# Attention followed by a max-out feed-forward: other wait points for the casting loads and for w_out, and a new planned order

## The chip, the cores and the metric

The kernel runs on one core of one Trainium2 chip. The core has a matrix engine (TensorE, PE in the profile), a vector engine (VectorE, DVE), a scalar engine (ScalarE, ACT), a general engine (GpSimd, POOL) and an engine that issues transfers (SyncE, SP). Each runs its own list of instructions in order; between lists they wait for each other through semaphores. Transfers between the chip's memory and the on-chip memory are issued from SP's, ACT's or POOL's list and run on 16 DMA engines. The metric is the time of one execution on the device in microseconds (us); lower is better.

## What is computed

Four batches, eight heads, 768 positions, head size 64. Three of the eight heads attend to all earlier positions; the other five see the first 4 positions and a window of 64. The heads' kinds are data (`is_retrieval`), so the kernel sorts the heads at run time. The joined heads (3072 x 512) go through a feed-forward with two up projections, of which the larger value is kept, and one down projection. The reference, cut:

```python
scores = scale * np.matmul(q, k.transpose(0, 1, 3, 2))
stream_keep = causal & (is_sink | in_win)
mask = np.where(retr[0, :, 0, 0, None, None], full_mask, stream_mask)
scores = np.where(mask[None, :, :, :], scores, -1000000000.0)
a = np.exp(scores - np.max(scores, axis=-1, keepdims=True))
a = a / (np.sum(a, axis=-1, keepdims=True) + 1e-09)
attn_out = np.matmul(a, v)
x = attn_out.transpose(0, 2, 1, 3).reshape(B * S, H * D)
g = np.maximum(x @ w1, x @ w2)
return g @ w_out
```

## The kernel before

**Tiling.** Each batch is cut into two halves of 384 positions, so there are eight half-batches (b, hf). Heads go in pairs: four pairs per half, one of two full heads, one mixed, two of streaming heads. Two heads of size 64 share the 128 rows of TensorE.

**Attention of one half.** q, k and v arrive as float32 in one of three landing slots (`ld`). q and k are cast to bfloat16 (`qb`, `CAST_QK`), turned on TensorE against an identity matrix (L813) and copied out (`qk`); v is cast (`vb`, `CAST_V`). TensorE makes scores (list S, L1027, with mask terms by L996 for the first half only), ACT takes the exponential (`at`, L1046), DVE multiplies masks (L1065), TensorE makes the weighted sums (list W, L1090), and DVE divides by the row sums (`x`, L1117). `x` is turned on TensorE for batch 0 (list TX, L1210) and by a transposing transfer later (`xt`, L1229).

**Feed-forward.** max(h1, h2) is written as max(h1 - h2, 0) + h2. So the kernel makes `w12` = w1 - w2 (L1246, `sub`), the up product x·w12 (list F, L1301), its positive part `g` (L1325, L1327), and then the output as g·w_out + x·(w2·w_out) in one accumulation (L1351). For that it needs `w2o` = w2·w_out: w2 is cast (`w2b`), turned on TensorE (list P, L1262), copied out (`w2t`), and multiplied with w_out (list P2, L1280). P2 works quarter by quarter: quarter c of w_out meets quarter c of the turned w2, for the k chunks 0 to 2 in the order of the quarters, then chunk 3 for all quarters.

**Loads of the front.** `LOADS` names the order: A and B are q and k of the two halves of batch 0, Av and Bv their v (three pieces each, by position), w20 and w21 the halves of w2, w10 and w11 those of w1. These are issued by SP. wo0 to wo3 are the quarters of w_out; they are cast on their way and issued by POOL. `load_down` (L696) makes each of them wait for an earlier load, `flow[-1 - PACE:len(flow) - PACE]` (L725): the list `flow` holds the earlier SP loads, and PACE is how far back from its end the awaited one lies. Before the wo quarters there stands a one-element copy on POOL (L701, tile `landed`), which is what waits. w1 uses the landing slot that A has left, and so waits for A's casts.

**The last batch.** Batch 3 is not cast by an engine. `load_pair` (L630) issues from POOL, for each pair and head, a casting load of q, k and v (24 in all, L648); q and k are then turned by a transposing transfer (L662). Ahead of the first stands again a one-element copy on POOL (L645) that waits for the load named by `BEHIND` = (half, kind) of batch 2; kind 1 is k, 2 is v.

**The order.** Nothing runs in program order. Each operation has a cost for every engine that could do it, operands and a rank (`RANK`; for batch 0 with `FRONT` and `FRONT_STEP` added; a shift by `STEP` for each half and `FF_STEP` for the feed-forward). While the kernel is built, a planner (`Order.run`, L206) plays the operations through in modelled time, gives each to the engine that would end it first (with a `BIAS` in us against an engine), and writes the instructions in that order. TensorE's work is in lists of fixed inner order (`PE_LISTS`); between lists it takes the first that is ready, a `MARGIN` after it became ready, and, if nothing is, a product on a zero tile (L514, tile `warmer`) up to `WARM_UNTIL`. Scores of a half may begin once the weighted sums of pair `S_AFTER` of the previous half have begun (L1146).

```python
behind = loads[b - 1, BEHIND[0], BEHIND[1]][-1:] if BEHIND else []
wo_in[c] = load_down(c, flow[-1 - PACE:len(flow) - PACE])
deps.append(first_w[(b, 0, S_AFTER) if hf else (b - 1, 1, S_AFTER)])
return begins + o.costs[e2] + o.bias.get(e2, 0.0)
```

Of the kernel before, what the change touches and what calls it, by code (L numbers as in the profile page):

```python
# [132 lines left out]
class Order:  # L133
# [256 lines left out]
CAST_QK = {'POOL': 0.46, 'DVE': 0.27, 'ACT': 0.4}  # L390
CAST_V = {'POOL': 0.3, 'DVE': 0.26, 'ACT': 0.26}
RANK = {
    'cast': -0.9, 'vcast': 14.25, 'unturn': 5.45, 'mix_k': 2.0, 'mix_v': -15.1, 'exp': -2.35,
    'mask': -2.15, 'norm': -12.35, 'take_x': -2.05, 'turn': -22.0, 'w2b': -17.35, 'sub': -9.15,
    'w2t': -3.85, 'wob': 0.35, 'w2o': -6.05, 'relu': 7.1, 'load': 6.6, 'out': -9.7, 'h2': 7.4,
    'table': -10.6, 'vload': 14.1,
}
NLD = 3
NQB = 4
# [8 lines left out]
PE_LISTS = ('TX', 'W', 'S', 'TK', 'TQ', 'P', 'H', 'P2', 'F')  # L408
PLACES = (0, 1, 2, 0, 1, 2, 0, 1, 2, 0, 1, 2, 0, 1, 2, 0, 1, 2, 0, 1, 2, 0)
SECOND_UP = False  # L410
LOADS = ('A', 'B', 'Av', 'w20', 'wo0', 'wo1', 'wo2', 'wo3', 'w10', 'w21', 'w11', 'Bv')
BIAS = {'DVE': 0, 'ACT': 0}
BIAS_MIX = {}
W2B_BEHIND = True
NORM = {'DVE': 0.35}
TURNED_BY_DMA = ()
DMA_TURN = 0.25
PACE = 1
W2O_EARLY = 3
X_LAST = ((0, 0),)  # L420
BIASED = ((0, 0),)
# [15 lines left out]
    0.22, 'six': 0.37,  # L437
}
SPARE = {}
STEP = 0.5  # L440
FF_STEP = -8.1
S_AFTER = 3
S_RUN = 2
S_REST = 1
ENTER_S = 0.1
# [2 lines left out]
COLD_UNTIL = 7.5  # L448
WARM_SHARE = 0.9
SHARE = {'S': 0.45, 'W': 0.8}  # L450
MARGIN = {'W': 0.5, 'S': 2.0, 'F': 0.2, 'TQ': 2.0}
X_MARGIN = 0.4
FRONT = (
    {'mix_k': -15.0, 'mask': 45.1, 'unturn': -38.9, 'exp': 16.6, 'vcast': 17.6, 'cast': -78.7,
    'norm': 6.4}, {'vcast': 14.0, 'unturn': -14.2, 'exp': 51.8, 'mask': 26.2, 'norm': -7.5,
    'mix_k': 24.9, 'cast': 21.2},
)
FRONT_STEP = (31.9, 11.4)
UNTURN_BIAS = ({}, {'ACT': 2.0})
SHARED = 0.89  # L460
UP_PARTS = 2
BY_ACT = {}
V_QUEUES = ()
BEHIND = (1, 2)


def tile_three_full_heads(
# [12 lines left out]
    ident, bias, smask = tab[:, 0:128], tab[:, 128:1152], tab[:, 1152:1920]  # L480
# [39 lines left out]
    T = {}  # L520

    def copy(e, out, in_):
        if e == "ACT":
            nc.scalar.copy(out=out, in_=in_)  # L524
        else:
            eng[e].tensor_copy(out=out, in_=in_)  # L526
# [146 lines left out]
    def load_up(name, src, c):  # L673

        if name not in T:
            s, old, tenants[name] = slot()
            staged_old[name] = old
            T[name] = lds[:, s].rearrange("p t h c -> p (t h c)")[:, 0:KC * d_ff] \
                .rearrange("p (c f) -> p c f", f=d_ff)
        n = d_ff // UP_PARTS  # L680

        by_act = name[:2] + str(c) in BY_ACT

        def emit(_):
            queues["ACT" if by_act else "SP"].dma_start(
                out=T[name][:, :, c * n:c * n + n],
                in_=src.rearrange("(c p) f -> p c f", p=128)[:, :, c * n:c * n + n],
            )
        return dma(
            2.097 / UP_PARTS, emit, [order.given(BY_ACT[name[:2] + str(c)])] if by_act else (),  # L690
            old=staged_old[name], rate=RATE["w"] if UP_PARTS == 4 else RATE["w half"],
            parts=1536 // UP_PARTS, grain=180.0 / UP_PARTS, rank=-9.0 if by_act else 0.0,
            by="ACT" if by_act else "SP",
        )

# [15 lines left out]
    slot_of, tenants, bias_in, table_in, staged_old, half_old, place_of = {}, {}, [], [], {}, {}, {}  # L711
    w1_in, w2_in, wo_in, flow = {}, {}, {}, []
    for what in LOADS:
        kind, c = what[:2], int(what[2:]) if what[:1] == "w" else 0
        if what[0] in "ABCD":
            kinds = (2,) if what[1:] else (0, 1)
            of = divmod("ABCD".index(what[0]), 2)
            load_half(*of, kinds)
            flow += loads[(*of, kinds[-1])]
            for n, o in enumerate(loads[(*of, kinds[-1])]):  # L720
                last = (n if kinds[-1] == 2 or of not in LONG else NT - 1) * D
                row = 64 if kinds[-1] == 1 and of in SIX else 0
                place_of[o] = row, lds[row:row + 1, slot_of[of], kinds[-1], 0, last:last + 1]
        elif kind == "wo":
            wo_in[c] = load_down(c, flow[-1 - PACE:len(flow) - PACE])  # L725
        else:
            got, src = (w1_in, w1) if kind == "w1" else (w2_in, w2)
            got[c] = load_up(kind + "f", src, c)
            flow.append(got[c])
            place_of[got[c]] = 0, T[kind + "f"][0:1, 0, c * d_ff // UP_PARTS:c * d_ff // UP_PARTS + 1]  # L730
    registers = order.given(REGISTERS)
    bias_in.append(order.given(MASKS_MADE))

# [154 lines left out]
    def prepare(b, hf, p):  # L888
# [7 lines left out]
        else:  # L896
# [4 lines left out]
            for hh in range(2):  # L901
                for lo, hi in ((0, 1), (1, 2)) if (b, hf) in SPLIT and (b, hf) not in SIX else ((0, 2),):
# [336 lines left out]
    def prep_weights():  # L1239
        sub_ops, w2b_ops, w2t_ops, w2o_ops = [], [], [], []  # L1240
        n = d_ff // 4
        for c in range(4):
            at = slice(c * n, c * n + n)
            sub_ops.append(op(
                {"DVE": 1.15},
                lambda e, at=at: eng[e].tensor_tensor(  # L1246
                    out=w12[:, :, at], in0=T["w1f"][:, :, at], in1=T["w2f"][:, :, at], op=ALU.subtract
                ),
                [w1_in[c * UP_PARTS // 4], w2_in[c * UP_PARTS // 4]], tag=f"sub{c}", rank=RANK["sub"], port=("POOL",),
            ))  # L1250
            w2b_ops.append(op(
                {"DVE": 0.61, "ACT": act(1024)},
                lambda e, at=at: copy(e, w2b[:, :, at], T["w2f"][:, :, at]), [w2_in[c * UP_PARTS // 4]],
                tag=f"w2b{c}", rank=RANK["w2b"], port=("DVE",),
            ))
            key = ("pw", c)

            def emit(_, c=c, key=key):
                pw = bank(key, BF16)
                for e in range(2 * KC):  # L1260
                    fc = 2 * c + e // KC
                    nc.tensor.transpose(  # L1262
                        pw[:, e * 128:e * 128 + 128],
                        w2b[:, e % KC, fc * 128:fc * 128 + 128], ident,
                    )

            def take(e, c=c, key=key):
                copy(e, w2t[:, 2 * c:2 * c + 2].rearrange("f c k -> f (c k)"), bank(key, BF16))
            o = pe("P", mm(*[128] * 2 * KC), emit, [w2b_ops[c]], claims=[(key, 1)])
            w2t_ops.append(op({"DVE": 0.62, "ACT": act(1024)}, take, [o], frees=[key], tag=f"w2t{c}", rank=RANK["w2t"]))  # L1270
        leaves("w2f", range(3), w2b_ops + sub_ops)
        leaves("w1f", range(3), sub_ops)
        steps = [(c, kc) for c in range(4) for kc in range(W2O_EARLY)]
        steps += [(c, kc) for kc in range(W2O_EARLY, KC) for c in range(4)]
        for c, kc in steps:
            key = ("pw2", kc)

            def emit(_, kc=kc, key=key, c=c):
                for fc in (2 * c, 2 * c + 1):
                    nc.tensor.matmul(  # L1280
                        bank(key), lhsT=w2t[:, fc, kc * 128:kc * 128 + 128], rhs=wob[:, fc, :],
                        start=(fc == 0), stop=(fc == FC - 1),
                    )
            o = pe(
                "P2", mm(512, 512), emit, [w2t_ops[c], wo_in[c]], claims=[(key, 1)] if c == 0 else [],
            )
            if c == 3:
                w2o_ops.append(op(
                    {"DVE": 0.6, "ACT": act(512)},
                    lambda e, kc=kc, key=key: copy(e, w2o[:, kc], bank(key)), [o], frees=[key],  # L1290
                    rank=RANK["w2o"],
                ))
        return sub_ops, list(wo_in.values()), w2o_ops
# [468 lines left out]
```

## Time and profile before

| | |
|---|---|
| median of 3 runs | 180.99 us (180.62 to 182.13) |
| the profiled execution | 180.24 us |
| its span | 178.6 us, 4964 instructions |
| granted TensorE clock | 0.997 |
| read from memory, written | 25.17 MB, 6.29 MB |
| DVE, ACT, POOL busy | 106.3, 129.5, 39.5 us |

The span is the time from the first to the last instruction; the profiled execution is 1.6 us longer than it. A row of a timeline or of the chain begins with the start and the length in us, then the engine, the line, the operation, what it writes and reads, and in brackets the idle time before it and what ended it. "q" behind an engine's name means its issuing part. A matmul's busy time overlaps the next one's, so the chain's lengths, and not the busy times, say how long a group held TensorE.

### The profile page before, as it was taken

The page shows a single profiled execution, that of the slowest core. Times are in us where ns is not written, and L with a number is a line of the kernel's source. Part 1 is how long each engine was busy: PE and PEld are TensorE (multiplying, and loading weights), DVE is VectorE, ACT ScalarE, POOL GpSimd, SP SyncE. Part 2 cuts the span into 40 slices and gives each one's busy share as a digit, 9 for nine tenths or more (in the row PEclk, how much of TensorE's full clock was granted, in tenths as well). Part 3 has the DMA queues.
Part 4 walks back from the last instruction along what each step waited for, and adds up shares of the span by engine and source line. Part 5 has one row for each costly group of instructions (what it writes and reads, how often), then busy time and mean ns, then how long its engine had stood idle before and what let it go on. Part 6 is the DMA issues. An engine that isn't in the chain of part 4 may idle for free.

```text
span 178.6 us, 4964 instructions
## 1 busy us (share of the span) xinstructions
PE 171.1 (96%) x1824; PEld 106.6 (60%) x1843; DVE 106.3 (60%) x319; ACT 129.5 (73%) x285; POOL 39.5 (22%) x75
## 2 busy tenths in 40 slices
PE   7898999999999999999999999999999999999991
PEld 7865985466746747666555655564465566545560
DVE  5487994699797999898673466664044176400000
ACT  3589897489599999899975996583283988425430
POOL 6313600050002605039997510000000000000000
PEclk9999999999999999999999999999999999999998
DMA  4999999999998999969999999991310511412022
GB/s 122 333 312 217 389 197 301 347 274 321 204 266 222 335 214 255 322 191 85 134 192 126 210 158 116 225 240 34 117 62 0 147 62 61 92 71 111 4 87 98
DMA packets 72529, 32.37 MB, mean 181 GB/s; under 512 B 53938, under 2 KB 67506, under 8 KB 72498
## 3 DMA queue, kind: packets, MB, share of 16 engines
q1 hardware_dynamic: 52448, 28.45, 63.0%
q0 software_dynamic: 19904, 3.41, 29.0%
q8 instruction: 16, 0.26, 0.6%
q14 instruction: 15, 0.12, 0.3%
q10 hardware_dynamic: 146, 0.13, 0.2%
HBM read 25.17 MB, written 6.29 MB: 176 GB/s over the span
## 4 chain that ended last, share of the span: by engine, by line
PE 93%; DVE 2%; issue 2%; ACT 1%; POOL 0%; DVEq 0%; ACTq 0%; POOLq 0%
PE ps L1351 35%; PE ps L1301 23%; PE ps L1027 10%; PE ps L1090 8%; PE ps L514 6%; PE ps L813 5%; PE ps L1280 4%; PE ps L996 1%; PE ps L1262 1%; PE ps L1210 1%; DVE vx L526 1%; DVE qk L526 1%; ACT qb L524 0%; DVE at L1065 0%; DVE x L1117 0%
## 5 line engine op out<-in xcount | busy, mean ns | idle before, releaser
L1046 ACT ACTIVATE at<-ps 128x512 bf16<-128x512 f32 (+2 forms) x134 | 64.3, 583 | 3.4 <-PE ps L1027 3.0
L1301 PE MATMUL ps<-xt,w 128*128 128x384 bf16 x256 | 46.1, 326 | 0.0
L1351 PE MATMUL ps<-wob,g 128*128 128x512 bf16 (+1 forms) x195 | 45.5, 370 | 0.2
L524 ACT COPY ot<-ps 128x512 f32<-128x512 f32 (+1 forms) x22 | 12.6, 573 | 28.0 <-PE ps L1351 28.0
L1301 PEld LDWEIGHTS <-w 128*128 128x128 bf16 x256 | 23.5, 98 | 14.7 <-issue 0.2
L1065 DVE TENSOR_TENSOR at<-at,tab 128x1024 bf16<-128x1024 bf16 (+5 forms) x49 | 24.2, 503 | 13.1 <-ACT at L1046 12.7
L1351 PEld LDWEIGHTS <-g 128*128 128x128 bf16 x200 | 18.6, 98 | 19.1 <-issue 0.2
L1325 ACT ACTIVATE g<-ps 128x384 bf16<-128x384 f32 x49 | 24.2, 507 | 5.2 <-PE ps L1301 4.7
L1351 PE MATMUL ps<-w2o,xt 128*128 128x512 bf16 (+1 forms) x89 | 23.6, 370 | 0.6
L1090 PEld LDWEIGHTS <-at 128*128 128x128 bf16 x477 | 19.4, 97 | 7.2 <-DVE at L1065 0.7
L1117 DVE TENSOR_TENSOR x<-ps,rez 128x192 f32 x64 | 22.7, 355 | 1.6
L1090 PE MATMUL ps<-vb,at 128*128 128x65 bf16 x387 | 21.1, 193 | 0.3 <-DVE at L1065 0.3
L1027 PE MATMUL ps<-qk 64*128 64x128 bf16 (+1 forms) x330 | 19.5, 228 | 0.1
L1027 PEld LDWEIGHTS <-qk 64*128 64x128 bf16 x330 | 12.3, 94 | 10.8 <-issue 8.2
L1327 DVE TENSOR_SCALAR g<-ps 128x384 bf16<-128x384 f32 x15 | 8.1, 552 | 11.2 <-PE ps L1301 10.9
L514 PE MATMUL ps<-warmer 128*128 128x128 bf16 x146 | 13.4, 252 | 1.2 <-POOL warmer L1695 1.2
L526 POOL CAST vb<-ld 128x192 bf16 x15 | 6.8, 493 | 33.6 <-DMA ld<-in_v_dram 32.4
L1351 PEld LDWEIGHTS <-xt 128*128 128x128 bf16 x100 | 8.8, 97 | 8.1 <-issue 0.2
L813 PE MATMUL ps<-tab,qb 128*128 128x128 bf16 x144 | 11.3, 221 | 1.2 <-ACT qb L524 0.5
L526 DVE CAST qb<-ld 128x384 bf16 (+1 forms) x34 | 11.0, 375 | 2.0 <-DMA ld<-in_q_dram 1.2
L514 PEld LDWEIGHTS <-warmer 128*128 128x128 bf16 x146 | 11.2, 116 | 1.6 <-POOL warmer L1695 1.2
L526 DVE COPY qk<-ps 128x384 bf16<-128x384 bf16 (+1 forms) x17 | 10.8, 666 | 2.1 <-PE ps L813 1.9
(72 smaller groups left out, 160.6 us busy)
## 6 DMA issues: line engine op xcount, KB each, us to landing
out_dram<-ot SPq DMA_DIRECT2D x23, 256.0 KB, 2.8
ld<-in_q_dram SPq DMA_DIRECT2D x6, 768.0 KB, 7.0
ld<-in_k_dram SPq DMA_DIRECT2D x6, 768.0 KB, 7.5
ld<-in_v_dram SPq DMA_DIRECT2D x18, 256.0 KB, 6.9
ld<-in_moe_w_dram SPq DMA_DIRECT2D x4, 1024.0 KB, 12.8
wob<-in_moe_w_out_dram POOLq DMA_DIRECT2D x4, 256.0 KB, 9.1
ld<-in_q_dram POOLq DMA_DIRECT2D x8, 96.0 KB, 7.8
ld<-in_k_dram POOLq DMA_DIRECT2D x8, 96.0 KB, 7.7
```

Of the source, the lines that this page charges most:

```text
L514: nc.tensor.matmul(banks[e][:, 0:128], lhsT=warm, rhs=warm, start=True, stop=True)
L524: nc.scalar.copy(out=out, in_=in_)
L526: eng[e].tensor_copy(out=out, in_=in_)
L813: nc.tensor.transpose(to[:, i], qbs[:, T["qb", n, hf] % NQB, t, i].rearrange("p h d -> p (h d)"), ident)
L1027: nc.tensor.matmul(to.rearrange("p (i c) -> p i c", c=128), lhsT=lhsT, rhs=q_of(n, i, m)[rows], start=bk not in under, stop=True, skip_gro ...
L1046: nc.scalar.activation(out=at[:, bk, 0:w], in_=bank(("ps", b, hf, t), part=bk)[:, 0:w], func=ACT.Exp, scale=scale,)
L1065: eng[e].tensor_tensor(out=at, in0=at, in1=tbl, op=ALU.mult)
L1090: nc.tensor.matmul(po[:, hh, i - NT * hf, :], lhsT=ats[:, T["at", b, hf, t] % NAT, bk, e * 128:(e + 1) * 128], rhs=rhs, start=first, stop= ...
L1117: nc.vector.tensor_tensor(out=xs[:, (2 * b + hf) % NX, :, bass.ds(heads[2 * p + hh], 1), :], in0=po[:, hh, :, 0:D].unsqueeze(2), in1=z[:, ...
L1301: nc.tensor.matmul(bank(key)[:, 0:HALF], lhsT=w[:, kc, fc * 128:(fc + 1) * 128], rhs=xts[:, (2 * b + hf) % NXT, :, kc, :], start=(kc == 0) ...
L1325: nc.scalar.activation(out=g, in_=ph, func=ACT.Relu)
L1351: nc.tensor.matmul(bank(key)[:, cols], lhsT=lhsT, rhs=(w2o if kind == "x" else wob)[:, c, cols], start=(e == 0), stop=(e == len(steps) - 1),)
```

## The change

It changes constants of the planner and waits, and adds a switch that is off (`W2_ROWS = False`: w2 loaded by rows instead of columns).

- The order of the front's loads: wo0 and wo1 are now named ahead of w20, w21 and w10, and wo2 and wo3 behind them. With PACE 2 instead of 1 the awaited load changes too. Before, all four waited for the last v piece of A (`flow` = A's k, B's k, three pieces of A's v, w20; the one before the last). After, wo0 and wo1 wait for the first v piece of A, and wo2 and wo3 for w20.
- SP's own order stays: w20, w21, w10, w11 and Bv, where w10 and w11 wait for A's landing slot and so came behind w21 before as well.
- BEHIND goes from (1, 2) to (1, 1): batch 3's casting loads wait for the load of k in the second half of batch 2. There k is followed by two v pieces.
- BIAS: the casts of batches 1 and 2 count 2.5 us more on DVE and ACT.
- S_AFTER, STEP, FF_STEP, MARGIN, RANK, FRONT, FRONT_STEP and UNTURN_BIAS get other values, so that the planner writes another order.

```diff
 RANK = {
-    'cast': -0.9, 'vcast': 14.25, 'unturn': 5.45, 'mix_k': 2.0, 'mix_v': -15.1, 'exp': -2.35,
-    'mask': -2.15, 'norm': -12.35, 'take_x': -2.05, 'turn': -22.0, 'w2b': -17.35, 'sub': -9.15,
-    'w2t': -3.85, 'wob': 0.35, 'w2o': -6.05, 'relu': 7.1, 'load': 6.6, 'out': -9.7, 'h2': 7.4,
-    'table': -10.6, 'vload': 14.1,
+    'cast': -0.7, 'vcast': 17.15, 'unturn': 4.4, 'mix_k': 0.3, 'mix_v': -16.2, 'exp': -2.7,
+    'mask': -2.3, 'norm': -10.5, 'take_x': -3.3, 'turn': -22.15, 'w2b': -16.6, 'sub': -10.25,
+    'w2t': -6.05, 'wob': -0.15, 'w2o': -7.05, 'relu': 6.15, 'load': 7.7, 'out': -11.0, 'h2':
+    7.3, 'table': -8.8, 'vload': 14.85,
 }
...
-LOADS = ('A', 'B', 'Av', 'w20', 'wo0', 'wo1', 'wo2', 'wo3', 'w10', 'w21', 'w11', 'Bv')
-BIAS = {'DVE': 0, 'ACT': 0}
+LOADS = ('A', 'B', 'Av', 'wo0', 'wo1', 'w20', 'w21', 'w10', 'wo2', 'wo3', 'w11', 'Bv')
+BIAS = {'DVE': 2.5, 'ACT': 2.5}
...
-PACE = 1
+PACE = 2
...
-STEP = 0.5
-FF_STEP = -8.1
-S_AFTER = 3
+STEP = 1.25
+FF_STEP = -7.8
+S_AFTER = 2
...
-MARGIN = {'W': 0.5, 'S': 2.0, 'F': 0.2, 'TQ': 2.0}
+MARGIN = {'W': 0.8, 'S': 0.1, 'F': 0.2, 'TQ': 2.0}
...
-    {'mix_k': -15.0, 'mask': 45.1, 'unturn': -38.9, 'exp': 16.6, 'vcast': 17.6, 'cast': -78.7,
-    'norm': 6.4}, {'vcast': 14.0, 'unturn': -14.2, 'exp': 51.8, 'mask': 26.2, 'norm': -7.5,
-    'mix_k': 24.9, 'cast': 21.2},
+    {'mix_k': -24.2, 'mask': 36.1, 'unturn': -31.6, 'exp': 21.0, 'vcast': 16.4, 'cast': -81.7,
+    'norm': 6.7}, {'vcast': 16.6, 'unturn': -20.3, 'exp': 50.8, 'mask': 26.2, 'norm': -4.7,
+    'mix_k': 31.8, 'cast': 10.7},
 )
-FRONT_STEP = (31.9, 11.4)
-UNTURN_BIAS = ({}, {'ACT': 2.0})
+FRONT_STEP = (28.1, 11.4)
+UNTURN_BIAS = ({'ACT': 1.0}, {})
...
-BEHIND = (1, 2)
+BEHIND = (1, 1)
+W2_ROWS = False
```

More of the change, by code (lines that the diff above doesn't have):

```diff
@@ L680, in load_up @@
         n = d_ff // UP_PARTS
+        by_rows = name == "w2f" and W2_ROWS
+        at = np.s_[:, 2 * c:2 * c + 2] if by_rows else np.s_[:, :, c * n:c * n + n]
         by_act = name[:2] + str(c) in BY_ACT
@@ L685, in emit @@
             queues["ACT" if by_act else "SP"].dma_start(
-                out=T[name][:, :, c * n:c * n + n],
-                in_=src.rearrange("(c p) f -> p c f", p=128)[:, :, c * n:c * n + n],
+                out=T[name][at], in_=src.rearrange("(c p) f -> p c f", p=128)[at],
             )
@@ L691, in load_up @@
             old=staged_old[name], rate=RATE["w"] if UP_PARTS == 4 else RATE["w half"],
-            parts=1536 // UP_PARTS, grain=180.0 / UP_PARTS, rank=-9.0 if by_act else 0.0,
+            parts=1536 // UP_PARTS, grain=156.0 if by_rows else 180.0 / UP_PARTS, rank=-9.0 if by_act else 0.0,
             by="ACT" if by_act else "SP",
@@ L729, in tile_three_full_heads @@
             flow.append(got[c])
-            place_of[got[c]] = 0, T[kind + "f"][0:1, 0, c * d_ff // UP_PARTS:c * d_ff // UP_PARTS + 1]
+            at = (2 * c, 0) if kind == "w2" and W2_ROWS else (0, c * d_ff // UP_PARTS)
+            place_of[got[c]] = 0, T[kind + "f"][0:1, at[0], at[1]:at[1] + 1]
     registers = order.given(REGISTERS)
@@ L1248, in prep_weights @@
                 ),
-                [w1_in[c * UP_PARTS // 4], w2_in[c * UP_PARTS // 4]], tag=f"sub{c}", rank=RANK["sub"], port=("POOL",),
+                [w1_in[c * UP_PARTS // 4], *(w2_in.values() if W2_ROWS else [w2_in[c * UP_PARTS // 4]])], tag=f"sub{c}", rank=RANK["sub"], port=("POOL",),
             ))
@@ L1252, in prep_weights @@
                 {"DVE": 0.61, "ACT": act(1024)},
-                lambda e, at=at: copy(e, w2b[:, :, at], T["w2f"][:, :, at]), [w2_in[c * UP_PARTS // 4]],
+                lambda e, at=np.s_[:, c] if W2_ROWS else np.s_[:, :, at]: copy(e, w2b[at], T["w2f"][at]),
+                [w2_in[c * UP_PARTS // 4]],
                 tag=f"w2b{c}", rank=RANK["w2b"], port=("DVE",),
@@ L1260, in emit @@
                 for e in range(2 * KC):
-                    fc = 2 * c + e // KC
+                    fc, kc = (e, c) if W2_ROWS else (2 * c + e // KC, e % KC)
                     nc.tensor.transpose(
                         pw[:, e * 128:e * 128 + 128],
-                        w2b[:, e % KC, fc * 128:fc * 128 + 128], ident,
+                        w2b[:, kc, fc * 128:fc * 128 + 128], ident,
                     )
             def take(e, c=c, key=key):
+                if W2_ROWS:
+                    src = bank(key, BF16).rearrange("f (c k) -> f c k", k=128)
+                    copy(e, w2t[:, :, c * 128:c * 128 + 128], src)
+                    return
                 copy(e, w2t[:, 2 * c:2 * c + 2].rearrange("f c k -> f (c k)"), bank(key, BF16))
@@ L1274, in prep_weights @@
         steps += [(c, kc) for kc in range(W2O_EARLY, KC) for c in range(4)]
+        if W2_ROWS:
+            early = min(W2O_EARLY, 2)
+            steps = [(c, kc) for c in range(4) for kc in range(early)]
+            steps += [(c, kc) for kc in range(early, KC) for c in range(4)]
         for c, kc in steps:
@@ L1284, in prep_weights @@
             o = pe(
-                "P2", mm(512, 512), emit, [w2t_ops[c], wo_in[c]], claims=[(key, 1)] if c == 0 else [],
+                "P2", mm(512, 512), emit, [w2t_ops[kc if W2_ROWS else c], wo_in[c]], claims=[(key, 1)] if c == 0 else [],
             )
```

## The prediction

> **What bounds the kernel now.** I read the page first (busy shares and the chain by line), then the chain in order of time, then each engine's timeline in the front part.
>
> ```profile
> span 178.6 us, 4964 instructions
> PE 171.1 (96%) x1824; PEld 106.6 (60%) x1843; DVE 106.3 (60%) x319; ACT 129.5 (73%) x285; POOL 39.5 (22%) x75
> ...
> PE ps L1351 35%; PE ps L1301 23%; PE ps L1027 10%; PE ps L1090 8%; PE ps L514 6%; PE ps L813 5%; PE ps L1280 4%; PE ps L996 1%; PE ps L1262 1%; PE ps L1210 1%; DVE vx L526 1%; DVE qk L526 1%; ACT qb L524 0%; DVE at L1065 0%; DVE x L1117 0%
> ```
>
> TensorE is the bound: 96% busy and nearly the whole chain. One entry is no work: L514 at 6%, matmuls on a zero tile that fill time in which no product is ready. Real work cannot shrink here, because the change leaves every product in place. So the question is how much of TensorE's time in the front is filler or stall, and whether a new stall opens behind it. How full it is behind the front, by stretches:
>
> ```profile
> 25.50:35.50 10.00, 9.89 (x93) 5.55 (x93) 5.80 (x11) 6.87 (x15) 0.00 (x0) 1.00 1.14 310
> ...
> 60.00:80.00 20.00, 19.84 (x237) 12.53 (x239) 18.79 (x58) 18.97 (x38) 4.61 (x10) 1.00 0.99 259
> ...
> 153.90:175.00 21.10, 20.86 (x115) 11.14 (x115) 0.63 (x5) 7.81 (x16) 0.00 (x0) 1.00 0.26 86
> ```
>
> The columns are the stretch, its length, busy time of PE, PEld, DVE, ACT and POOL, the granted clock, the DMA share and GB/s. TensorE is idle 0.1 to 0.25 us in each of these stretches, at full clock; in the last one DVE works 0.63 us, so little but feed-forward products is left. Nothing is to be won behind the front. In 60 to 80, though, DVE (18.79 of 20) and ACT (18.97) are almost full, which is where a loss could start. The chain in the front:
>
> ```profile
> 23.12 1.34 PE ps L514 x24
> 24.46 0.71 PE ps L1027 x14
> ...
> 25.21 0.33 PE ps L514 x3
> 25.54 0.45 PE ps L1262 x8
> ...
> 26.25 0.61 PE ps L1262 x8
> 26.86 0.67 PE ps L1210 x12
> 27.53 1.29 PE ps L1280 x6
> 28.82 0.71 PE ps L1027 x9
> 29.53 2.91 PE ps L1280 x13
> ...
> 33.09 0.78 PE ps L1027 x24
> 33.87 1.83 PE ps L1280 x8
> 35.70 3.92 PE ps L1301 x24
> ```
>
> The last filler is 1.34 and 0.33 us at 23 to 25.5 us. The products w2·w_out (L1280) begin only behind it, end at 35.70, and the first feed-forward (L1301) follows at once. Why they begin so late:
>
> ```profile
> 17.40 0.18 POOL L701 COPY landed<-ld 1x1 f32<-1x1 f32 x1 [3.00 <-DMA ld<-in_v_dram]
> 17.52 0.84 POOL L702 DMA_DIRECT2D wob<-in_moe_w_out_dram  x1
> ...
> 37.73 2.30 POOL L526 CAST vb<-ld 128x192 bf16 x4 [16.87 <-DMA ld<-in_v_dram]
> ```
> ```profile
> wob<-in_moe_w_out_dram POOLq DMA_DIRECT2D x1, 256.0 KB, 7.9
> ```
> ```profile
> 20.62 1.05 ACT L524 CAST w2b<-ld 128x1024 bf16<-128x1024 f32 x1 [0.33 <-DMA ld<-in_moe_w_dram]
> ```
> ```profile
> 22.78 0.69 DVE L526 COPY w2t<-ps 128x1024 bf16<-128x1024 bf16 x1
> ```
>
> GpSimd waits 3.00 us for the last v piece of half A and issues the first quarter of w_out at 17.52; it lands 7.9 us later, at 25.4. The turned w2 that the same product needs is ready at 23.5 (22.78 + 0.69). So w_out is the operand that comes last, by about 1.9 us.
>
> **The change, part by part.**
>
> *w_out's quarters 0 and 1* now wait for A's first v piece:
>
> ```profile
> 6.10 6.93 SPq L597 DMA_DIRECT2D ld<-in_v_dram  x3
> ```
> ```profile
> ld<-in_v_dram SPq DMA_DIRECT2D x1, 256.0 KB, 8.4
> ```
>
> That one is issued at 6.10 and lands 8.4 later, at 14.5, against 17.4 for the last: issued 2.9 us sooner, quarter 0 lands at about 22.5 and 1 about a microsecond behind. Then 12 products (two quarters, three k chunks each) of 0.224 us (2.91 / 13) are ready from 23.5: 2.7 us of work for the 1.67 us of filler. The gain is at most 1.67. It is capped by what the first feed-forward waits for, w1's first half and the subtraction:
>
> ```profile
> ld<-in_moe_w_dram SPq DMA_DIRECT2D x1, 1024.0 KB, 12.8
> wob<-in_moe_w_out_dram POOLq DMA_DIRECT2D x1, 256.0 KB, 11.3
> ```
> ```profile
> 20.23 2.92 SPq L685 DMA_DIRECT2D ld<-in_moe_w_dram  x2
> ```
> ```profile
> 33.74 2.35 DVE L1246 TENSOR_TENSOR w<-ld 128x1024 bf16<-128x1024 f32 x2
> ```
>
> w1 lands at 20.23 + 12.8 = 33.0, one subtraction is 1.18 (2.35 / 2), so the feed-forward may start at about 34.4 with some 0.2 for the hand-over, 1.3 sooner than 35.70. I take 1.2 off; the ends are 0 and 1.67.
>
> *Quarters 2 and 3* wait for w2's first half, which landed just ahead of its cast at 20.62. Two issues and two one-element copies put them at about 20.8 and 21.7, 1.5 us later than now. GpSimd has nothing else until 37.73 (idle 16.87), so nothing is queued behind that wait. Landing by the 11.3 of the last quarter is 32.1 and 33.0; with two quarters already out of the way, by 9.5 (its forerunner's time halfway between the 7.9 and the 11.3, an estimate), 30.3 and 31.2. TensorE's cover between the early products' end, at about 26.2, and 30.3 is L1262, L1210 and three runs of L1027: 0.45 + 0.61 + 0.67 + 0.71 + 0.71 + 0.78 = 3.9 of 4.1 us. So 0.2 is added; the ends are 0 and 1.8 (32.1 less 30.3).
>
> *Batch 3's casting loads* wait for the third batch's k, not its last v:
>
> ```profile
> 69.87 0.43 SPq L584 DMA_DIRECT2D ld<-in_k_dram  x1
> ```
> ```profile
> ld<-in_k_dram SPq DMA_DIRECT2D x1, 768.0 KB, 7.1
> ```
> ```profile
> 79.30 0.31 POOL L645 COPY landed<-ld 1x1 f32<-1x1 f32 x1 [1.28 <-DMA ld<-in_v_dram]
> ```
>
> k lands at 77.0, so the 24 loads begin up to 2.3 us sooner. I cost this at nothing: TensorE is as full before these loads (the row from 60) as after batch 3's attention (the row from 153.9), and batch 3's scores lie among feed-forward work. If the earlier loads slow the last v pieces, their casts come later by at most the same 2.3, under that same cover.
>
> *The plan.* A bias of 2.5 us against DVE and ACT sends batch 1 and 2's casts to GpSimd until its backlog is that long; the margins and ranks let scores start sooner. Each cast by engine:
>
> ```profile
> L526 DVE CAST qb<-ld x22: 348/352/660, 44.1 to 79.8; 128x384 bf16 x22
> L524 ACT CAST qb<-ld x7: 501/551/562, 43.2 to 79.6; 128x384 bf16 x7
> L526 POOL CAST qb<-ld x3: 631/667/928, 55.6 to 77.1; 128x384 bf16 x3
> ```
>
> If some 20 of the 29 move, DVE and ACT are relieved by about 20 x 0.4 = 8 us and GpSimd takes 20 x 0.667 = 13.3, which it has free (4.61 us busy of 20 in the row from 60). TensorE feels neither while it is full, so 0, with ends of -0.9 and +3.2, both worked out below. The branches on W2_ROWS are off and cost nothing.
>
> Sum: -1.2 + 0.2 + 0 + 0 = -1.0. The profiled execution was 180.24 (span 178.6 and 1.6 around it), so it would be 179.2; the median of the runs, 180.99, stands 0.75 above it and gives **180.0**.
>
> **The rivals.**
>
> *More is won.* All 1.67 us of filler goes, with 0.7 more where half B's weighted sums now stall, at 39.67 and 42.35:
>
> ```profile
> 39.67 0.44 issue
> ...
> 42.35 0.58 DVE at L1065
> ```
>
> The relief of DVE shortens that chain, and a few score runs fewer make up the rest: -2.4, 178.6. Against it: B's last v comes when it came, whatever the weights do.
>
> *The front does not move.* Quarters 0 and 1 now share the transfer engines with w2's first half, which is what their products need too. They move 310 GB/s at that time, with a share of 1.14 (the row from 25.5). The two quarters are 1.05 MB in f32, 3.4 us at that rate. If half of that goes ahead of w2, it lands 1.7 us later and the filler stays: 181.0. [...] The trace leans toward it only partly: the w1 half that shared its way with all four quarters took 12.8 us.
>
> *Slower.* Batch 1's first eight q/k casts are made side by side now:
>
> ```profile
> 43.16 1.79 ACT L524 CAST qb<-ld 128x384 bf16 x4
> ```
> ```profile
> 44.09 1.16 DVE L526 CAST qb<-ld 128x384 bf16 x4
> ```
>
> Both are done by 45.3, 2.1 us after the start. On GpSimd alone eight take 8 x 0.667 = 5.3, 3.2 later. The turns and scores of that half slip by as much; from the point where TensorE has run out of the previous half's feed-forward, it shows. One such half costs 3.2: 180.0 + 3.2 = 183.2. For it: DVE's cast took 660 ns at worst beside 352. Against it: one half's down products alone are 36 x 0.224 (L1280's, of the same width) = 8.1 us of cover. [...]
>
> **How the numbers follow.** Forecast (179.2 to 180.7): 0.48. More won, 178.6: 0.20. Front unmoved, 181.0: 0.18. Slower, 183.2: 0.14. Over 1%, which is what a measurement here can tell from no change, means below 179.2 or above 182.8. Faster: 0.20 and 0.02 of the forecast's edge, 0.22; slower: most of its case, 0.12; within: 0.66. The range 178.3 to 182.3 holds three cases and leaves out the fourth and the far side of the second.
>
> **What would show it.** Right: the first w_out issue near 14.6, L1280 beginning near 23.5 with no L514 behind it, L1301 beginning at 34.4 to 34.8, TensorE as full as now from 43 on, batch 3's first load near 77 with no effect. Wrong: a w2 cast clearly after 20.62, L514 left between 23 and 30, L1301 still at 35.7; or TensorE idle behind casts on GpSimd between 45 and 85.

## The result, and the profile after

| | before | changed |
|---|---|---|
| median | 180.99 us (21 runs) | 179.91 us (21 runs) |
| ratio to before | | 0.9929, 95% interval 0.9908 to 0.9950 |
| profiled execution, its span | 180.24, 178.6 | 180.37, 178.7 |

The kernel became 0.7% faster, about 1.3 us. The two spans do not show it: the execution profiled before lies 0.75 us below its median, the one profiled after 0.46 above. So the time of the whole kernel is taken from the ratio, and the traces are compared place by place. Two more profiles of the changed kernel (below: 179.48 and 179.52 us, both with a span of 177.9) stand beside the first. Of the 0.8 us between their spans and the first one's, 0.4 and 0.6 stand already at the first up product (below). The granted clock has no part in it: its mean is 0.996 in the first and 1.000 in the others, but in the first it reads 1.00 in every stretch up to 177 us and falls only behind the last product, which ends at 175.0 us (0.66 from 177 to 178, 0.50 from there on). Ratios compare undisturbed executions; others take 1 to 6 us more, some of them at a lower granted clock (0.991 in the two traces that the last section follows), and some at full clock (181.46 us at 1.000), for a reason that no trace shows.

Line numbers have moved: L514 is now L515, L1280 L1291, L1262 L1265, L1301 L1312, L1351 L1362, L813 L815, L1246 L1248, L1027 L1029, L1090 L1092, L526 L527; the rest by 1 to 11. The page of the changed kernel:

```profile
PE 171.3 (96%) x1837; PEld 106.7 (60%) x1837; DVE 99.1 (55%) x286; ACT 124.0 (69%) x268; POOL 60.2 (34%) x125
...
PE ps L1362 35%; PE ps L1312 24%; PE ps L1092 8%; PE ps L1029 7%; DMA wob<-in_moe_w_out_dram 6%; DMA ld<-in_moe_w_dram 4%; SPq L598 4%; PE ps L815 3%; SPq L585 3%; PE ps L1291 1%; DVE w L1248 1%; POOL qb L527 1%; POOL landed L702 0%; DVE w2o L527 0%; PE ps L1212 0%
```

TensorE is still the bound. In the chain's list the filler is no longer named: up to 32 us the chain now runs through the issues of q, k and v and the transfers of w2 and w_out, and later, also new, through casts on GpSimd (POOL qb L527). The filler itself is still there. The products on the zero tile by stretches, the kernel before first (the first number behind the length is TensorE's busy time):

```profile
6.80:17.00 10.20, 3.05 (x32) 2.17 (x33) 0.00 (x0) 1.00 1.11 269
17.00:25.50 8.50, 4.68 (x67) 3.70 (x64) 0.00 (x0) 1.00 1.10 314
```
```profile
6.80:17.00 10.20, 5.63 (x60) 3.83 (x60) 0.00 (x0) 1.00 1.09 271
17.00:25.50 8.50, 1.83 (x21) 1.25 (x21) 0.00 (x0) 1.00 1.11 313
```

There are 28 more ahead of 17 us, where TensorE idled 1.31 us and now 0.25, and 46 fewer from 17 to 25.5. But there it now idles 0.73 us instead of 0.04, ahead of the first turns of w2. GpSimd's timeline in the front, and TensorE's (start, length, engine, line, what, idle before):

```profile
14.60 0.18 POOL L702 COPY landed<-ld 1x1 f32<-1x1 f32 x1
14.72 0.92 POOL L703 DMA_DIRECT2D wob<-in_moe_w_out_dram  x1
...
20.71 0.63 POOL L702 COPY landed<-ld 1x1 f32<-1x1 f32 x1 [4.22 <-DMA ld<-in_moe_w_dram]
...
22.12 0.72 POOL L703 DMA_DIRECT2D wob<-in_moe_w_out_dram  x1
```
```profile
23.97 1.03 PE L1291 MATMUL ps<-wob,w2t 128*128 128x512 bf16 x4
...
26.30 0.44 PE L515 MATMUL ps<-warmer 128*128 128x128 bf16 x5
...
27.04 0.62 PE L1265 MATMUL ps<-tab,w2b 128*128 128x128 bf16 x8
...
32.02 3.18 PE L1291 MATMUL ps<-wob,w2t 128*128 128x512 bf16 x14 [0.60 <-DMA wob<-in_moe_w_out_dram]
35.39 2.77 PE L1312 MATMUL ps<-xt,w 128*128 128x384 bf16 x16 [0.19 <-DVE w L1248]
...
42.56 1.89 PE L1362 MATMUL ps<-wob,g 128*128 128x512 bf16 x8
```

Quarter 0 is issued at 14.72 instead of 17.52, and the products with w_out begin at 23.97 instead of 25.82. But they pause for 0.60 us at 32.0, where the last quarter lands. The first up product begins at 35.39, only a little before the 35.54 of the old kernel. The two other profiles of the changed kernel have no such pause (their last quarter lands at 31.1 and 31.3), and there it begins sooner:

```profile
35.02 1.15 PE L1312 MATMUL ps<-xt,w 128*128 128x384 bf16 x6 [0.19 <-DVE w L1248]
```
```profile
34.78 1.47 PE L1312 MATMUL ps<-xt,w 128*128 128x384 bf16 x8 [0.19 <-DVE w L1248]
```

So 0.15, 0.52 and 0.76 us are won ahead of the feed-forward. The old kernel's rows for the stretch behind it:

```profile
35.54 4.71 PE L1301 MATMUL ps<-xt,w 128*128 128x384 bf16 x28
...
41.88 0.81 PE L1301 MATMUL ps<-xt,w 128*128 128x384 bf16 x4
42.98 0.20 PE L1090 MATMUL ps<-vb,at 128*128 128x65 bf16 x1 [0.29 <-DVE at L1065]
...
43.45 1.67 PE L1351 MATMUL ps<-wob,g 128*128 128x512 bf16 x7
```

From the first up to the first down product it was 7.91 us, and is now 42.56 - 35.39 = 7.17. Not all of these 0.74 us is won. In the old order eight more weighted sums (8 x 0.03 = 0.24 us) stand in this stretch; in the new order they come behind the first down products. The stall of 0.29 us ahead of them is gone. The last 0.2 us is the length of one down product, of which the old row has 7 and the new one 8, so probably a record is missing. That leaves about 0.3 us won behind the start of the feed-forward. Later, near 77 us, part is lost again:

```profile
60.00:80.00 20.00, 19.24 (x240) 12.33 (x239) 14.95 (x41) 18.70 (x39) 14.02 (x32) 1.00 1.13 274
```
```profile
75.38 4.59 POOL L527 CAST qb<-ld 128x384 bf16 x8 [3.39 <-PE ps L1029]
79.90 0.18 POOL L646 COPY landed<-ld 1x1 f32<-1x1 f32 x1
80.03 0.84 POOL L649 DMA_DIRECT2D ld<-in_q_dram  x1
```
```profile
77.76 0.51 PE L815 MATMUL ps<-tab,qb 128*128 128x128 bf16 x6 [0.76 <-POOL qb L527]
```

The first of these rows is the stretch table again: TensorE is busy 19.24 of 20 us where it was 19.84. It stands still for 0.76 us ahead of the turns of batch 2's second half, behind casts that GpSimd now makes.

These places do not add up to 1.3 us: the two profiled executions are 0.13 us apart, the wrong way round, and the rest is how far each lies from its median.

### The profile page after: what moved, and what is told of

Same layout as the page of the kernel before. It is cut to its first block, busy times and chain, and to the rows that moved or that the text cites. A ratio compares the mean times of both kernels' runs of the same rounds, so it can differ in the third digit from the quotient of the medians.

```text
span 178.7 us, 4988 instructions
## 1 busy us (share of the span) xinstructions
PE 171.3 (96%) x1837; PEld 106.7 (60%) x1837; DVE 99.1 (55%) x286; ACT 124.0 (69%) x268; POOL 60.2 (34%) x125
## 4 chain that ended last, share of the span: by engine, by line
PE 78%; DMA 10%; SPq 7%; POOL 1%; DVE 1%; issue 1%; ACT 0%; POOLq 0%
PE ps L1362 35%; PE ps L1312 24%; PE ps L1092 8%; PE ps L1029 7%; DMA wob<-in_moe_w_out_dram 6%; DMA ld<-in_moe_w_dram 4%; SPq L598 4%; PE ps L815 3%; SPq L585 3%; PE ps L1291 1%; DVE w L1248 1%; POOL qb L527 1%; POOL landed L702 0%; DVE w2o L527 0%; PE ps L1212 0%
## 5 line engine op out<-in xcount | busy, mean ns | idle before, releaser
L1048 ACT ACTIVATE at<-ps 128x512 bf16<-128x512 f32 (+2 forms) x134 | 65.2, 581 | 7.7 <-PE ps L1029 7.6
L1362 PE MATMUL ps<-wob,g 128*128 128x512 bf16 (+1 forms) x200 | 47.3, 371 | 0.0
L1312 PE MATMUL ps<-xt,w 128*128 128x384 bf16 x256 | 45.4, 326 | 0.2 <-DVE w L1248 0.2
L1067 DVE TENSOR_TENSOR at<-at,tab 128x1024 bf16<-128x1024 bf16 (+5 forms) x49 | 25.4, 524 | 14.8 <-ACT at L1048 14.3
L1312 PEld LDWEIGHTS <-w 128*128 128x128 bf16 x256 | 23.8, 98 | 15.8 <-DVE w L1248 0.7
L1336 ACT ACTIVATE g<-ps 128x384 bf16<-128x384 f32 x53 | 26.2, 500 | 7.0 <-PE ps L1312 6.7
L1362 PEld LDWEIGHTS <-g 128*128 128x128 bf16 x200 | 18.1, 98 | 17.1
L527 POOL CAST qb<-ld 128x384 bf16 (+1 forms) x41 | 19.7, 535 | 17.7 <-PE ps L1092 6.0
L1362 PE MATMUL ps<-w2o,xt 128*128 128x512 bf16 (+1 forms) x100 | 24.8, 371 | 0.0
L1092 PEld LDWEIGHTS <-at 128*128 128x128 bf16 x477 | 20.0, 97 | 7.7 <-issue 0.6
L1092 PE MATMUL ps<-vb,at 128*128 128x65 bf16 x387 | 21.3, 193 | 0.0
L1029 PE MATMUL ps<-qk 64*128 64x128 bf16 (+1 forms) x330 | 19.2, 228 | 0.0
L527 POOL CAST vb<-ld 128x192 bf16 x34 | 13.1, 452 | 17.9 <-DMA ld<-in_v_dram 17.7
L1029 PEld LDWEIGHTS <-qk 64*128 64x128 bf16 x330 | 12.1, 94 | 8.7 <-issue 6.1
L515 PE MATMUL ps<-warmer 128*128 128x128 bf16 x140 | 13.9, 253 | 1.2 <-POOL warmer L1706 1.2
L1362 PEld LDWEIGHTS <-xt 128*128 128x128 bf16 x100 | 9.2, 98 | 9.0 <-issue 0.2
L1338 DVE TENSOR_SCALAR g<-ps 128x384 bf16<-128x384 f32 x11 | 6.0, 556 | 13.7 <-PE ps L1312 12.9
L815 PE MATMUL ps<-tab,qb 128*128 128x128 bf16 x144 | 12.4, 220 | 1.0 <-POOL qb L527 1.0
L1109 DVE RECIPROCAL rez<-ps 128x6 f32<-128x6 f32 x32 | 5.3, 188 | 14.0 <-PE ps L1092 13.5
L515 PEld LDWEIGHTS <-warmer 128*128 128x128 bf16 x140 | 11.1, 117 | 1.7 <-POOL warmer L1706 1.2
```

Of the source, the lines that this page charges most:

```text
L515: nc.tensor.matmul(banks[e][:, 0:128], lhsT=warm, rhs=warm, start=True, stop=True)
L815: nc.tensor.transpose(to[:, i], qbs[:, T["qb", n, hf] % NQB, t, i].rearrange("p h d -> p (h d)"), ident)
L1029: nc.tensor.matmul(to.rearrange("p (i c) -> p i c", c=128), lhsT=lhsT, rhs=q_of(n, i, m)[rows], start=bk not in under, stop=True, skip_gro ...
L1048: nc.scalar.activation(out=at[:, bk, 0:w], in_=bank(("ps", b, hf, t), part=bk)[:, 0:w], func=ACT.Exp, scale=scale,)
L1067: eng[e].tensor_tensor(out=at, in0=at, in1=tbl, op=ALU.mult)
L1092: nc.tensor.matmul(po[:, hh, i - NT * hf, :], lhsT=ats[:, T["at", b, hf, t] % NAT, bk, e * 128:(e + 1) * 128], rhs=rhs, start=first, stop= ...
```

## The experiments

Theory A: the gain is w_out's first two quarters coming sooner, and part of it is lost near 77 us. Theory B: the gain is the new plan elsewhere, DVE and ACT being relieved of casts. The experiments on the waits change no instruction's place in any engine's list; they change only which landing a one-element copy waits for (one of them drops two copies).

**The changed kernel again.**

> The changed kernel unaltered, for a second profile. Both theories: 179.9 within 0.4. Theory A (w_out's first quarters, landing sooner, let L1291 replace filler; a share of that is lost again behind batch 2's casts on GpSimd): the first L1291 near 24.0 us against 25.8 before, and an idle TensorE ahead of an L815 near 77 us that differs from run to run between 0 and 1 us, as k of batch 2's second half lands sooner or later. Theory B (the gain is that of the new order elsewhere, DVE and ACT being relieved of casts): no stall, and the gain appears after 60 us.

> The changed kernel unaltered, beside the two others: 179.9 within 0.4. Theories A and C: the pause near 77 us again, of a size that goes with the landing of k and xt. Theory B: none.

Measured: 179.85 us, ratio 0.9893 (0.9838 to 0.9949), and 180.19, 0.9931 (0.9899 to 0.9963). Idle TensorE time between 74 and 83 us, from the stretch tables: 0.54 and 1.05 us, 0.76 in the first profile, none before. The pause is there each time and its size varies, as A has it. Only in two of the three is it behind casts on GpSimd, though; in the 0.54 us TensorE waited for the transposing transfer (`xt`).

**All four quarters wait as before, in the new order.**

```diff
-            for o in behind:
+            for o in loads[0, 0, 2][-1:]:
```

> The new order instruction for instruction; only the four w_out quarters wait again for the last v piece of half A. Theory A: quarter 0 lands near 25.4 instead of 23.0, TensorE stands still ahead of L1291 near 24 us for 1 to 1.5 us, quarters 2 and 3 land about 2 us sooner and the 0.6 us wait at 32 us goes: net 0.4 to 1.0 slower than the changed kernel, 180.3 to 180.9. Theory B: 179.9 within 0.3.

Measured: 188.31 us, ratio 1.039 (1.0351 to 1.0428). This miss has a cause of its own. The place that the copy reads, A's v, had by then been given to w1, so the copy for quarter 2 waited for w1:

```profile
30.80 0.17 POOL L702 COPY landed<-ld 1x1 f32<-1x1 f32 x1 [11.47 <-DMA ld<-in_moe_w_dram]
```

The run therefore does not show the old waits; it shows mainly what quarters 2 and 3 cost when they come 10 us late. The next one is free of this.

**Only quarters 0 and 1 wait as before, in the new order.**

```diff
-            for o in behind:
+            for o in loads[0, 0, 2][-1:] if c < 2 else behind:
```

> The new order; only quarters 0 and 1 wait again for A's last v piece, quarters 2 and 3 keep their new wait. Theory A: quarter 0 lands near 25.4 instead of 23.3, TensorE stands still ahead of the first L1291 for 1.3 to 1.6 us; 1 to 1.6 slower than the changed kernel (180.9 to 181.5), and 3 or more slower if the pause is long enough to halve the granted clock. Theory B (w_out's wait is not where the gain is): 179.9 within 0.3.

Measured: 180.61 us, ratio 0.9993 (0.9970 to 1.0017): the gain is gone. The row of TensorE that it stands on:

```profile
25.34 1.02 PE L1291 MATMUL ps<-wob,w2t 128*128 128x512 bf16 x3 [1.17 <-DMA wob<-in_moe_w_out_dram]
```

TensorE waits 1.17 us for quarter 0, and the first up and down products come at 36.28 and 43.45, each 0.89 later than in the first profile of the changed kernel (1.26 and 1.50 later than in the others at the first up product). Against 0.9929 this wait is worth 0.64%, or 1.16 us of 181; by the two intervals, 0.6 to 1.7. B falls as the cause of the gain. In this profile TensorE idles only 0.16 us between 74 and 83: the pause near 77 us comes where TensorE is early there, so the 1.16 us is probably what is left of the front's gain behind it.

**The new waits in the old order.**

```diff
-            for o in behind:
+            for o in loads[0, 0, 2][:1] if c < 2 else [w2_in[0]]:
```

> The old order instruction for instruction; quarters 0 and 1 wait for A's first v piece, quarters 2 and 3 for w2's first half. Theory A: the filler is written into the order ahead of L1280, so the sooner quarters find no use, and the later ones cost up to 0.6: 181.0 to 181.6. Rival (the waits alone make the gain): 179.9 within 0.4.

Measured: ratio 1.0059 (1.0028 to 1.0091), 1.1 us slower than before. The rival falls; A had 0 to 0.6 us, and for another reason than the trace shows (of an execution of 184.22 us, one of the longer ones):

```profile
27.26 1.03 PE L1262 MATMUL ps<-tab,w2b 128*128 128x128 bf16 x8 [1.85 <-DVE w2b L526]
```

w2's second half now shares its way with quarters 0 and 1 and lands 11.4 us behind its issue, 8.4 before. The old order has its turns (L1262) ahead of the products with w_out, and so TensorE waits 1.85 us for it, with work ready behind. The new order puts the products first. Neither the new waits in the old order (1.0059) nor the new order with the old wait for quarters 0 and 1 (0.9993) gains; together they give 0.9929.

**Quarters 2 and 3 wait for nothing.**

```diff
-            for o in behind:
+            for o in behind if c < 2 else []:
```

> The new order; quarters 2 and 3 wait for nothing and are issued right behind quarter 1, at about 16.5 instead of 21.3 us. If the wait for the last quarter (32.0 us) sets the first feed-forward, this ends w2 times w_out about a microsecond sooner, L1312 begins at 34.2 to 34.6 instead of 35.4 and the median falls by 0.4 to 1.0, to 178.9 to 179.5. If the transfers only change places, w2's second half lands 1 to 2 us later, L1265 with it, and the time is the changed kernel's or up to 1.5 more.

Measured: 180.08 us, ratio 0.9964 (0.9937 to 0.9992): no better than the changed kernel, on the side of the second expectation. w2's second half:

```profile
ld<-in_moe_w_dram SPq DMA_DIRECT2D x1, 1024.0 KB, 12.3
```
```profile
23.09 1.05 PE L1265 MATMUL ps<-tab,w2b 128*128 128x128 bf16 x16 [1.55 <-DVE x L1119]
...
28.40 0.62 PE L1265 MATMUL ps<-tab,w2b 128*128 128x128 bf16 x8 [0.43 <-DVE w2b L527]
...
36.10 1.15 PE L1312 MATMUL ps<-xt,w 128*128 128x384 bf16 x6 [0.19 <-DVE w L1248]
```

Issued at 15.30, it lands 12.3 us later, at 27.6, and both groups of turns come 0.9 and 1.4 us later than in the changed kernel. The cast of w2's first half, too, begins at 21.50 instead of 20.61. The first up product begins at 36.10, not 34.4. In the front the transfers only change places, so the later issue of quarters 2 and 3 loses nothing.

**Batch 3's loads wait as before.**

```diff
-                    for o in [] if T.get("last batch") else behind:
+                    for o in [] if T.get("last batch") else loads[b - 1, 1, 2][-1:]:
```

> The new order; batch 3's casting loads wait again for batch 2's last v piece. Theory A: GpSimd is busy with batch 2's casts until 79 to 80 us, by when that piece has landed too, so the first load comes within 0.5 us of where it came, and the time is 179.9 within 0.3. Rival (the wait in the change's title is worth something): the loads begin 1 to 2 us later, 0.5 to 1 slower.

Measured: 179.99 us, ratio 0.9942 (0.9912 to 0.9972), the same as with the new wait. The copy stood for 0.79 us, and the first load came at 80.52 instead of 80.03:

```profile
79.89 0.18 POOL L646 COPY landed<-ld 1x1 f32<-1x1 f32 x1 [0.79 <-DMA ld<-in_v_dram]
80.52 0.84 POOL L649 DMA_DIRECT2D ld<-in_q_dram  x1 [0.46 <-issue]
```

**Half of the casts back on DVE**, first for batch 2's second half alone, then for batches 1 and 2. Each cast keeps its place in the plan; only the engine that makes it is another.

```diff
+                    cast.really = {"POOL": "DVE"} if (b, hf) == (2, 1) and hh else {}
...
+                    cast.really = {"POOL": "DVE"} if b and hh else {}
```

> The new order; of the eight q/k casts of batch 2's second half, the four of the pairs' second heads are made by DVE instead of GpSimd. Theory A: the pause of 0.76 us ahead of L815 near 77 us goes down to 0.2 or less, and the median falls by 0.3 to 0.7 against the changed kernel, to 179.2 to 179.6. [...]

> The new order; of the 32 q/k casts of batches 1 and 2 that GpSimd makes, the 16 of the pairs' second heads are made by DVE. Theory A: which engine casts is of no account while TensorE is full: 179.9 within 0.4. Theory B (relieving DVE and ACT is the gain): half of it goes back, 180.3 to 180.6, with waits on DVE at L1092 or L1029.

Measured: 180.02 us, ratio 0.9931 (0.9901 to 0.9961), and 180.02, 0.9947 (0.9918 to 0.9975). Neither differs from the changed kernel by more than the noise (0.3% either way). On the time, then, the choice of engine is of no account that these runs could tell, as theory A had it of the second; of the first it had 179.2 to 179.6. For the pause the two profiles disagree. In the first, of an execution of 183.3 us, one of the longer ones, it came with half the casts on DVE too:

```profile
77.53 0.51 PE L815 MATMUL ps<-tab,qb 128*128 128x128 bf16 x6 [1.26 <-ACT at L1048]
78.74 0.50 PE L815 MATMUL ps<-tab,qb 128*128 128x128 bf16 x6 [0.70 <-DVE rez L1109]
```

Here GpSimd's first cast of this half began at 76.81, after 5.03 us of idle time that k's landing ended, at 76.7. In the second k landed at 74.1, and between 74 and 83 TensorE idled 0.16 us:

```profile
74.00:83.00 9.00, 8.84 (x112) 6.18 (x113) 7.29 (x21) 8.30 (x17) 8.80 (x13) 1.00 1.63 196
```

In these two the pause goes with k's landing and not with the engine that casts. k is not later than it was: in the kernel before it landed at 77.0. But there its turns came 4.5 us behind it, and in the changed kernel 1.2 us (76.50, k at 75.3):

```profile
81.52 1.51 PE L813 MATMUL ps<-tab,qb 128*128 128x128 bf16 x24
```

**The turns placed later**, by telling the planner that k takes longer.

```diff
-            mb = 1.572 if early_k and (b, hf) == (0, 0) else 0.786
+            mb = 1.572 if early_k and (b, hf) == (0, 0) else 1.3 if (b, hf, t) == (2, 1, 1) else 0.786
```

> The changed kernel, with the planner told that k of batch 2's second half takes 1.6 us longer to land; the order is the same up to there and puts that half's turns (L815) later behind it. If the pause near 77 us comes from turns that stand too close behind that landing, no pause over 0.3 us is left between 74 and 83, no execution has a halved clock there, and the median falls by 0.3 to 0.9, to 179.0 to 179.6. Rival: the pause is taken up by slack later, 179.9 within 0.3.

Measured: 180.20 us, ratio 0.9971 (0.9950 to 0.9992), a miss. TensorE still idles 0.61 us between 74 and 83, now behind masks on DVE (0.5 us at L1092). But the edit hardly moved what it was meant to move: the first two groups of turns stand at 76.38 and 77.70, in the changed kernel at 76.50 and 77.76. So the run does not tell what later turns would give.

**k behind the transposing transfer.** In the first profile of the changed kernel xt landed at 76.6, in the second at 77.5, and there the up products waited 0.54 us for it. SP's list:

```profile
68.08 0.63 SPq L585 DMA_DIRECT2D ld<-in_k_dram  x1
68.79 4.95 SPq L1231 DMA_TRANSPOSE xt<-x  x1
```

It is issued right behind the 768 KB of k and lands 7.8 us later (9.8 and 8.2 in the other profiles). In the kernel before it stood ahead of k and landed 3.8 us later:

```profile
64.98 1.70 SPq L1229 DMA_TRANSPOSE xt<-x  x1
```

The edit puts k and the last two v pieces behind it:

```diff
-                mb, emit, old=old[0:2] if six else old[t:t + 1],
+                mb, emit, x_ready[1, 0] if (b, hf, t) == (2, 1, 1) else (), old=old[0:2] if six else old[t:t + 1],
...
-                0.262, emit, old=old[t:t + 1],
+                0.262, emit, x_ready[1, 0] if (b, hf) == (2, 1) and i else (), old=old[t:t + 1],
```

> The changed kernel, but in batch 2's second half k and the last two v pieces are issued behind the transposing transfer of batch 1's first half (xt), which they slow now; the order is the same up to there. Theory C (the new order's loss near 77 us is the transfer queue: k and xt share it, and turns and up products stand right behind both): xt lands 2 us or more sooner than 77, no pause over 0.5 us is left between 74 and 83, the median falls by 0.3 to 0.8 to 179.1 to 179.6. Rival: k then lands later and the turns wait for that; 179.9 or up to 1 more.

> The kernel with k behind the transposing transfer once more, as it came out ahead of both: theory C 178.8 within 0.4 and a ratio to the kernel before of 0.985 to 0.990; if the first result was luck, 179.9 within 0.4 and 0.993.

Measured: 178.75 us, ratio 0.9874 (0.9844 to 0.9905), and again 178.95, 0.9883 (0.9863 to 0.9904). SP's list, and the stretches from 60 and from 74:

```profile
67.64 2.64 SPq L1231 DMA_TRANSPOSE xt<-x  x1
...
73.99 0.43 SPq L585 DMA_DIRECT2D ld<-in_k_dram  x1
```
```profile
60.00:80.00 20.00, 19.68 (x259) 12.72 (x261) 15.71 (x44) 18.99 (x40) 8.54 (x21) 1.00 0.97 238
74.00:83.00 9.00, 8.84 (x120) 5.70 (x120) 7.04 (x20) 8.16 (x19) 3.73 (x7) 1.00 0.81 207
```

TensorE idles 0.16 us in 74 to 83, against 0.54 to 1.05, and 0.46 in the repeat, none of it ahead of turns or up products. This version is about 1.2% under the kernel before, and under the changed one: 0.9874 and 0.9883 against 0.9929, just clear of the noise, and against the 0.9893 and 0.9931 of its repeats, which by themselves are not clear of it. C has the direction and has the gain too small (179.1 to 179.6). Why it gains is not shown. k ahead of it is not what makes xt slow, or not all: with k behind, it still took 7.2 and 7.0 us to land, though it landed sooner, at 74.8 and 75.7. k now lands at 79.1, and the planner puts its turns at 83.99, 7.5 us later than before the edit. Nor is it shown that the pause is what the new plan gave back: the profile with half of the casts on DVE in batches 1 and 2 has no such pause, and that kernel is no faster than the changed one (0.9947). A profile is one execution and does not tell how often the pause comes in the others.

## Why the prediction was right, point by point

**The bound.** TensorE was full behind the front before (19.84 of 20 us from 60 to 80) and is 96% busy after. Only the front could give.

**Quarters 0 and 1: -1.2 forecast, 1.16 us measured** (0.9993 less 0.9929; 0.6 to 1.7). The mechanism was right: quarter 0 was to be issued near 14.6 and was at 14.72; L1291 was to begin near 23.5 and did at 23.97. That the two sizes agree to 0.04 us is luck at this noise. The cap was of the right kind and set too early. I had the first up product move from 35.70 (35.54 by the timeline) to 34.4; it came at 35.39, 35.02 and 34.78. w1 landed at 32.9, as forecast (33.0), but on DVE a copy of w2·w_out stands ahead of the first subtraction, here in the second profile:

```profile
33.14 0.69 DVE L527 CAST w2o<-ps 128x512 bf16<-128x512 f32 x1 [0.94 <-PE ps L1291]
33.74 3.49 DVE L1248 TENSOR_TENSOR w<-ld 128x1024 bf16<-128x1024 f32 x3
```

It stood there in the kernel before too, at 33.13, and I had left it out. For the hand-over I had 0.2 us, which no run shows; where quarter 2 waited for w1, L1312 began 0.05 us behind the subtraction (44.29, 44.34). Behind the first up product I had given 0.7 us of stall to the rival "more is won". I had read it from the chain, which there follows DVE; TensorE itself idled 0.29 us between 35.5 and 43.4, and now not at all.

**Quarters 2 and 3: +0.2 forecast.** I had the last quarter land at 31.2; it landed at 22.12 + 9.9 = 32.0 in the first profile and at 31.1 and 31.3 in the others:

```profile
wob<-in_moe_w_out_dram POOLq DMA_DIRECT2D x1, 256.0 KB, 9.9
```
```profile
wob<-in_moe_w_out_dram POOLq DMA_DIRECT2D x1, 256.0 KB, 9.0
```

So the forecast held in two executions of three. In the first, the late landing cost 0.60 us of pause. My end of +1.8 had room for it.

**Sharing with w2.** The rival "the front does not move" expected w2's first half to come 1.7 us later. Its cast began at 20.61, and at 20.62 before: not delayed. The second half, issued at 15.08, landed 11.2 us later instead of 8.4 after 15.20:

```profile
ld<-in_moe_w_dram SPq DMA_DIRECT2D x1, 1024.0 KB, 11.2
```

That is 26.3 instead of 23.6. So the delay fell on the load issued next, 2.7 us of it; the rival had a delay of w2 right and the half that it fell on wrong. That 1.7 of the quarters' 3.4 us would go ahead of w2 was my assumption: the traces show no delay for the first half, which had been issued at 13.03, 1.7 us ahead of quarter 0, and 2.7 us for the second, issued 0.4 us behind it. In the old order with the new waits the second half was delayed too, 11.4 us against 8.4. With quarters 2 and 3 early as well, the first half came 0.9 us later too.

**Batch 3's loads: nothing forecast, nothing measured.** But I had the first load near 77, and it came at 80.03. I had left out that the casts sent to GpSimd stand ahead of it in the same list, until 79.97.

**The casts: nothing forecast, nothing measured** when half of them go back. A loss came where my list of wrong signs had it, TensorE idle behind casts on GpSimd between 45 and 85, but not from the cause I gave the slower rival. The eight casts took 4.59 us instead of 5.3, and cost nothing at batch 1's first half (TensorE is busy 16.60 of 16.60 us from 43.4 to 60); the pause came at batch 2's second half, where k and xt land close ahead of the work that needs them.

**The sum.** -1.0 forecast, -1.3 measured (0.9 to 1.7): right, and in part by luck. Several signs went the wrong way: seven fillers (L515) still stand between 23 and 30 us, the first up product came later than 34.8 in two profiles of three, and the pause near 77 us, 0.54 to 1.05 us, I had not counted at all. Without the wait of quarters 0 and 1 everything else in the change comes to -0.1 us (0.9993; -0.5 to 0.3), against the +0.2 forecast. How much of the pause is in the medians is open.

## What to carry to other kernels

One load issued sooner can make another later: here, at a DMA share of 1.11 (17 to 25.5 us), quarters 0 and 1 went out 2.8 and 2.7 us sooner, and w2's second half landed 2.7 us later. Look up which load is next in the queue, and whether the order of work has something to do while that one is late. A wait and the order around it are one change; here neither the new waits in the old order nor the new order with the old wait gained. Work that a plan puts close behind a landing stalls when the landing comes late: here the turns 4.5 us behind k's landing showed no pause, and those 1.2 us behind it one of up to 0.85 us. And profile a changed kernel more than once: the pause at 32 us that seemed to set the start of the feed-forward stood in one execution of three.

## What the hardware showed that was not expected

In two experiments (half of the last casts on DVE; the new waits in the old order) a pause of TensorE cost more than its length. In their stretch tables the granted clock, the third number from the end, falls behind the pause:

```profile
75.30:79.00 3.70, 1.74 (x15) 0.86 (x16) 2.25 (x7) 2.69 (x6) 2.19 (x5) 1.00 0.90 180
79.00:82.50 3.50, 3.50 (x18) 1.72 (x16) 2.56 (x8) 2.05 (x5) 3.50 (x6) 0.57 1.50 240
82.50:86.00 3.50, 3.50 (x48) 2.72 (x47) 2.60 (x5) 2.60 (x5) 3.50 (x5) 0.94 1.86 122
```
```profile
26.50:30.00 3.50, 2.74 (x20) 2.19 (x21) 2.25 (x4) 1.26 (x3) 0.00 (x0) 0.59 1.14 279
30.00:33.00 3.00, 3.00 (x30) 1.86 (x28) 1.97 (x4) 0.73 (x2) 0.00 (x0) 0.91 1.06 386
```

In the first, pauses of 1.26 and 0.70 us left TensorE busy 1.74 of 3.70 us. Behind them 0.43 x 3.5 + 0.06 x 3.5 = 1.7 us of clock are missing; in the second, behind one pause of 1.85 us, 0.41 x 3.5 + 0.09 x 3.0 = 1.7 again. The run in which quarter 2 waited for w1, with a pause of 5.6 us, shows it at 0.50:

```profile
34.00:37.00 3.00, 0.28 (x1) 0.10 (x1) 0.00 (x0) 0.00 (x0) 0.69 (x2) 0.63 1.20 229
37.00:41.00 4.00, 4.00 (x24) 1.66 (x23) 0.00 (x0) 0.00 (x0) 0.00 (x0) 0.50 1.04 331
41.00:45.00 4.00, 3.81 (x18) 1.55 (x16) 2.54 (x3) 1.76 (x3) 2.34 (x3) 0.92 0.06 20
```

It lost 0.37 x 3.0 + 0.50 x 4.0 + 0.08 x 4.0 = 3.4 us of clock, twice the 1.7, but up to 1.1 of it within the pause itself. At the 0.50 of this run, 1.7 us would be a stretch of 3.4 us, an estimate: no trace shows where the lower clock begins and ends. Pauses of 0.76 us, of 1.17, and of 1.55 with 0.43 five microseconds later stand in executions with a mean clock of 0.996, 1.000 and 0.997, against 0.991 in the two above and 0.982 here. How long a pause has to be, these runs do not tell more closely. Where k came latest, at 76.7 us, with half of the last casts on DVE, the pause near 77 us was thus dearer than its length, and that execution took 183.3 us.
